# A spectral filter's 32-point transforms moved from TensorE to VectorE, inside an attention kernel

## The chip, the cores and the metric

One core of a Trainium2 chip. The metric is the device time of one execution in microseconds (us), the median of several runs. The engines run side by side and wait for one another by semaphores: TensorE (PE in the profile, its weight loads PEld), VectorE (DVE), ScalarE (ACT), GpSimd (POOL) and SyncE (SP), which here only issues DMAs.

## The reference

Two independent branches on 2048 x 448 inputs in float32, put side by side in the output: attention of 16 heads of 28 that share one key and one value head, and a filter in the frequency domain.

```python
def _A_ref(x, wq, wk, wv, wo):
    q = (x @ wq).reshape(B, S, H, Dh).transpose(0, 2, 1, 3)
    k = x @ wk
    v = x @ wv
    scores = jnp.einsum("bhqd,bkd->bhqk", q, k) * (Dh ** -0.5)
    p = _softmax(scores, axis=-1)
    o = jnp.einsum("bhqk,bkd->bhqd", p, v)
    return o.transpose(0, 2, 1, 3).reshape(B, S, H * Dh) @ wo

def _B_ref(x, w_r, w_i):
    X = jnp.fft.rfft2(x, axes=(-2, -1))
    X = X * (w_r + 1j * w_i)
    return jnp.fft.irfft2(X, (S, D), axes=(-2, -1))
```

The inputs A_wq and A_wk are drawn eight times as large as the other weights.

## The kernel before, in words

**Head.** TensorE projects x to queries, keys and values in four column chunks c of 512 queries, each in four groups g of four heads. Floats are split into a high and a low part and multiplied in two or three passes. Between the projections lie the first transforms of the filter (`fft1_fold`, `fft1_a`, `fft1_mm`, `fft1_out`), in eight portions q: the sequence of 2048 is cut into 64 x 32, and this step does the 448-point transform along the rows and the 64-point transform along the sequence. The result goes to the tile bs, and from there with two DMAs per q to the DRAM tensor t1. The keys are built in two halves (`keys(0)`, `keys(1)`), each moved into the tile ka by three DMAs. In the head only TensorE's order is written out; the order of the other engines and of SP's queue is made by the framework, by readiness and place in the program.

**Attention.** 16 groups (c, g), each of 16 steps (kc, 128 keys): 256 steps. A step is four score products into four PSUM banks (L696, out of a ring of six), four exponentials on ScalarE (L700) into tiles p, and four value products that run side by side in four column blocks of one bank, po (L678). TensorE does two steps of scores, then two steps of values. At the end of a group po is copied by VectorE (L686) and normalized in four parts (`norm`): the sum in every 29th row is spread over its 32 rows by a shuffle, inverted at full size and multiplied. `build_q` makes the next group's queries by three VectorE operations and nine DMAs. PSUM has eight banks: six for scores, one for fillers (aux), one for po.

**Fillers.** Between the scores of a pair of steps TensorE takes one unit of other work, by a table (`mid`, `at`): first the filter's 32-point transforms, forward (`fft2_a`) and back (`fft2_b`) as products with a 128 x 128 matrix in three split passes, the product with the filter on VectorE between them; from t1 and to t2, both in DRAM. Then the last transforms (`fft3_a`, `fft3_b`, from t2 to the output ob), and for each chunk c the output projection (`wo_unit`, L598) in 16 units. The last chunk's projection and the last group's normalization form the tail.

Of the kernel before, what the change touches and what calls it, by code (L numbers as in the profile page):

```python
# [1 line left out]

# [18 lines left out]
DH = D // H  # L21
DF = D // 2 + 1
NG = 4
# [5 lines left out]
BANKS = 6  # L29
O_BUFS = 1  # L30
X_BUFS = 1
P_BUFS = 8
LAG = 1
TAIL = 0
# [4 lines left out]
def kernel(ctx: ExitStack, tc: tile.TileContext, t: dict):  # L39
# [4 lines left out]
    dp = ctx.enter_context(tc.tile_pool(name="dp", bufs=1, space=DRAM))  # L44
    fp = ctx.enter_context(tc.tile_pool(name="fp", bufs=2))
    qp = ctx.enter_context(tc.tile_pool(name="qp", bufs=2))
# [11 lines left out]
    t1 = dp.tile([128, 32, DF], F32, name="t1")  # L58
    t2 = dp.tile([128, 32, DF], F32, name="t2")

# [6 lines left out]
    aux_pool = [None]  # L67

    def aux(name):
        return aux_pool[0].tile([128, 512], F32, name=name, tag="aux")  # L70

    def aux2(name):
        return aux_pool[0].tile([128, 2, DF], F32, name=name, tag="aux")

    fc, xb, ff = {}, {}, {}
    ps1 = [None]

    def fft1_consts():
        fc["cs1"] = fp.tile([128, 4, 113], F32, name="cs1", tag="cs", bufs=1)
        nc.sync.dma_start(fc["cs1"], t["cs1"])

    def fft1_load(q):
        if q > 7:
            return
        x = fp.tile([128, 4, 256], F32, name="xb", tag=("wr", "b2")[q % 2])
        nc.sync.dma_start(x, t["xb"][q])
        w = fp.tile([128, 4, 64], F32, name="fw", tag=("fi", "z0")[q % 2])  # L90
        nc.sync.dma_start(w, t["fw"][:, 4 * q:4 * q + 4])
        xb[q] = x, w

    def fft1_fold(q):
        x = xb[q][0][:113]
        f = ff[q] = fp.tile([113, 4, 4, 2, 32], F32, name="f", tag="wi")
# [12 lines left out]
    at1, stored = {}, []  # L109

    def fft1_a(q, ps=range(2)):
        f, cs1 = ff[q], fc["cs1"][:113]
        for p in ps:
            pa = ps1[0].tile([128, 2, DF], F32, name="pa", tag="p")
# [7 lines left out]
            a = at1[q, p] = fp.tile([128, 2, DF], F32, name="a", tag=("pwr", "pwi")[p])  # L122
            nc.scalar.activation(a, pa, AF.Copy)
# [4 lines left out]
    def fft1_mm(q):  # L128
        w = xb[q][1]
        pb = aux2("pbb"), ps_o.tile([128, 2, DF], F32, name="po")  # L130
# [8 lines left out]
    def fft1_out(q, pb, after=None):  # L139
        bs = fp.tile([128, 2, 2, DF], F32, name="bs", tag=("cst", "cst", "wr", "b2")[q // 2])  # L140
# [7 lines left out]
        for e in range(2):  # L148
            n0 = 16 * e + 2 * q
            stored.append(nc.sync.dma_start(t1.rearrange("(l s) n f -> s l n f", l=2)[:, :, n0:n0 + 2],  # L150
                                            bs[64 * e:64 * e + 64]))

    def fft2_consts():
        for n in ("g1", "g2"):
            g = fp.tile([128, 128], F32, name=n, tag="g", bufs=1)
            nc.gpsimd.dma_start(g, t[n])
            h = fc[n + "h"] = fp.tile([128, 128], F32R, name=n + "h", bufs=1)
            l = fc[n + "l"] = fp.tile([128, 128], F32R, name=n + "l", bufs=1)
            nc.gpsimd.tensor_copy(h, g)
            nc.gpsimd.tensor_tensor(l, g, h.bitcast(F32), op=ALU.subtract)  # L160

    qa = {}
# [10 lines left out]
    def build_q(c, g, first=False):  # L173
        cs = slice(c * CW, (c + 1) * CW)
        qt = qp.tile([128, CW], F32, name="qt", bufs=1)
        qh = qp.tile([128, CW], F32R, name="qh", bufs=1)
        ql = qp.tile([128, CW], F32R, name="ql", bufs=1)
# [3 lines left out]
        if (c, g) not in qa:  # L181
            qa[c, g] = qp.tile([128, 4, CW], F32R, name="qa")
        q = qa[c, g]
        if first:
            return q, qh, ql
        for i in range(4):
            for p, src in enumerate((qh, ql)):
                mv = nc.sync.dma_start(q[32 * p:32 * p + 32, i].bitcast(F32), src[32 * i:32 * i + 32].bitcast(F32))
                behind(mv, stored[-1])
# [3 lines left out]
    ps_x = ctx.enter_context(tc.tile_pool(name="ps_x", bufs=X_BUFS, space=PSUM))  # L193
    ps_o = ctx.enter_context(tc.tile_pool(name="ps_o", bufs=O_BUFS, space=PSUM))
    aux_pool[0] = ps_x


    with tc.tile_pool(name="w1", bufs=1) as w1, tc.tile_pool(name="p1", bufs=6, space=PSUM) as p1:
        ps1[0] = p1
# [30 lines left out]
        def shift(c0, c1):  # L230
            pb = p1.tile([128, NG, c1 - c0], F32, name="pb2", tag="p")
# [4 lines left out]
        with tc.tile_pool(name="x1", bufs=2) as x1:  # L236
# [6 lines left out]
            for n in WARM:  # L243
                nothing = p1.tile([128, 512], F32, name="nothing", tag="p")
# [54 lines left out]
            slots = (3, 5, 6, 8, 9, 10)  # L299
# [6 lines left out]
            def key_max():  # L306

                nc.vector.tensor_reduce(qm, qmx[:, 0:2], axis=AX.X, op=ALU.max)
                pb = p1.tile([128, 64], F32, name="pb", tag="p")
# [5 lines left out]
            pqs = [p1.tile([128, 512], F32, name="pq", tag="p") for _ in range(NG)]  # L315
# [16 lines left out]
            sgn = const("sgn", [128, 1], nc.sync)  # L332
# [7 lines left out]
            for c in range(1, NC):  # L340
                for g in range(NG):
                    pq = p1.tile([128, 512], F32, name="pq", tag="p")
# [22 lines left out]
                    if n in slots:  # L365
                        q = slots.index(n)
# [24 lines left out]
        pb3 = p1.tile([128, 64], F32, name="pb3", tag="p")  # L391
# [6 lines left out]
        pv = p1.tile([128, 16, 32], F32, name="pv", tag="p")  # L398
# [8 lines left out]
        with tc.If(rv > int(np.float32(BOUND).view(np.int32))), tc.tile_pool(name="g1", bufs=1) as g1:  # L407
# [9 lines left out]
            banks = [p1.tile([128, 512], F32, name="ps", tag="p") for _ in range(2)]  # L417
            with tc.For_i(0, 64, 1) as n:
# [3 lines left out]
                for i in range(4):  # L422
                    r = slice(32 * i, 32 * i + 32)
                    for h in range(4):
                        ps = banks[0]
                        mm(ps, qs[r], k4[r, h * 512:(h + 1) * 512], start=True, stop=True)
                        nc.vector.tensor_reduce(mx[:, i, h:h + 1], ps, axis=AX.X, op=ALU.max)
# [21 lines left out]
    ps_s = ctx.enter_context(tc.tile_pool(name="ps_s", bufs=1, space=PSUM))  # L449
    ring = [ps_s.tile([128, CW], F32, name=f"s{i}") for i in range(BANKS)]  # L450
# [3 lines left out]
    begun = []  # L454
    woh = ap.tile([128, NG, D], F32R, name="woh", bufs=1)
    wol = ap.tile([128, NG, D], F32R, name="wol", bufs=1)

    def wo_split(g):
        w = ap.tile([128, D], F32, name="wo", tag="ya")
        behind(nc.gpsimd.dma_start(w, t["wo"][:, g]), begun[-1])  # L460
# [4 lines left out]
    def mm3(out, w, h, l):  # L465
        mm(out, fc[w + "h"], h, start=True, stop=False)  # L466
        mm(out, fc[w + "l"], h, start=False, stop=False)  # L467
        mm(out, fc[w + "h"], l, start=False, stop=True)  # L468

    b2 = {}  # L470

    t1v = t1.rearrange("(l r h) n f -> r l n h f", r=2, l=2)

    def fft2_load(q):
        b = b2["b", q] = fp.tile([128, 4, DF], F32R, name="b2", tag="b2")
        for r in range(2):
            for l in range(2):
                p = (r * 2 + l) * 32
                ld = nc.sync.dma_start(b[p:p + 32].bitcast(F32), t1v[r, l][:, 4 * q:4 * q + 4])
                behind(ld, begun[-1])  # L480
        for n in ("wr", "wi"):
            b2[n, q] = fp.tile([128, 4, DF], F32, name=n)
            for r in range(2):
                ld = nc.gpsimd.dma_start(b2[n, q][64 * r:64 * r + 64], t[n][:, 4 * q:4 * q + 4])
                behind(ld, begun[-1])

    pr, cst = {}, {}

    def fft2_split(u):
        q, v = divmod(u, 2)  # L490
        b = b2["b", q][:, 2 * v:2 * v + 2]
        bh = b2["h", u] = fp.tile([128, 2, DF], F32R, name="bh", bufs=1)
        nc.vector.tensor_copy(bh, b.bitcast(F32))  # L493
        nc.vector.tensor_tensor(b, b.bitcast(F32), bh.bitcast(F32), op=ALU.subtract)

    def fft2_a(u):
        q, v = divmod(u, 2)
        s = slice(2 * v, 2 * v + 2)
        b, wr, wi = (b2[n, q][:, s] for n in ("b", "wr", "wi"))
        pu = aux2("pu")  # L500
        mm3(pu, "g1", b2["h", u], b)
        pf, p2 = fp.tile([128, 2, DF], F32, name="pwr"), fp.tile([128, 2, DF], F32, name="pwi")
        nc.vector.tensor_tensor(pf, pu, wr, op=ALU.mult)
        nc.vector.tensor_tensor(p2[0:64], pu[64:128], wi[64:128], op=ALU.mult)
        nc.vector.tensor_tensor(p2[64:128], pu[0:64], wi[0:64], op=ALU.mult)
        nc.vector.scalar_tensor_tensor(pf, p2, sgn, pf, op0=ALU.mult, op1=ALU.add)
        h = fp.tile([128, 2, DF], F32R, name="ph", bufs=1)
        nc.vector.tensor_copy(h, pf)
        p = fp.tile([128, 2, DF], F32R, name="pl", bufs=1)
        nc.vector.tensor_tensor(p, pf, h.bitcast(F32), op=ALU.subtract)  # L510
        pr[u] = h, p

    def fft2_b(u):
        v = u % 2
        pc = aux2("pc")
        mm3(pc, "g2", *pr.pop(u))
        if v == 0:
            cst[0] = fp.tile([128, 4, DF], F32, name="cst")
        nc.vector.tensor_copy(cst[0][:, 2 * v:2 * v + 2], pc)
        if v:  # L520
            nc.sync.dma_start(t2[:, 2 * u - 2:2 * u + 2], cst[0])


    def fft3_consts():
# [330 lines left out]
```

## Time and profile before

| what | value |
|---|---|
| median of three runs | 671.88 us (671.17 to 674.48) |
| span of the profiled execution | 669.5 us |
| TensorE busy | 660.4 us, 4480 products |
| ScalarE busy | 560.4 us |
| VectorE busy | 319.8 us |
| GpSimd busy | 63.4 us |
| DMA | 61.86 MB, 34250 packets |
| granted TensorE clock | 1.000 |

The span runs from the first to the last instruction of one profiled execution; the runs' times are taken without the profile and hold what lies around the span too. A line of a timeline has the start, the duration and the engine, then the program's line, the operation, the tiles (written <- read), the shape and the number of instructions that were merged, and in brackets the idle time before it with the one who ended it. SPq marks a DMA issue on SP's queue: the duration is that of the issue, not of the transfer. In the groups of lines the last columns are the busy time, the mean ns of one, and the idle time of the engine just before.

### The profile page before, as it was taken

What the parts mean: (1) busy time and instruction counts of PE and PEld (TensorE: products, weight loads), DVE (VectorE), ACT (ScalarE), POOL (GpSimd) and SP (SyncE); (2) the same over time, 40 slices, a digit from 0 to 9 for tenths busy, and PEclk for the clock granted to TensorE, in tenths of its full rate; (3) what the DMA queues carried; (4) which work ended last, traced back from release to release, by engine and by line L of the source; (5) the groups of instructions that cost most, each with busy time, mean ns of one, the idle gap of its engine ahead of it and who ended that gap; (6) DMA issues with size and microseconds to landing.
All of it is one profiled execution on the core that took longest, in us unless ns stands there. A gap on an engine that the chain in (4) does not pass through costs nothing.

```text
span 669.5 us, 11846 instructions
## 1 busy us (share of the span) xinstructions
PE 660.4 (99%) x4480; PEld 371.3 (55%) x4480; DVE 319.8 (48%) x771; ACT 560.4 (84%) x1117; POOL 63.4 (9%) x113
## 2 busy tenths in 40 slices
PE   8999899999999999999999999999999999999997
PEld 6877545555555555555555555555555555555555
DVE  5999537759995912045342502073514220071613
ACT  4554898988988988988898988899898998898882
POOL 3022202322110000000001100000100100000110
PEclk9999999999999999999999999999999999999999
DMA  8765755656452323030322222020423220120001
GB/s 261 257 170 169 208 147 140 146 149 163 136 139 83 79 83 78 15 77 15 83 80 60 74 70 54 22 70 15 121 56 89 77 69 23 46 60 1 28 29 56
DMA packets 34250, 61.86 MB, mean 92 GB/s; under 512 B 6529, under 2 KB 22802, under 8 KB 33228
## 3 DMA queue, kind: packets, MB, share of 16 engines
q1 hardware_dynamic: 30544, 49.18, 26.6%
q0 software_dynamic: 3072, 11.00, 6.4%
q8 instruction: 36, 0.59, 0.4%
q10 hardware_dynamic: 576, 0.92, 0.4%
q14 instruction: 22, 0.18, 0.1%
HBM read 29.35 MB, written 14.75 MB: 66 GB/s over the span
## 4 chain that ended last, share of the span: by engine, by line
PE 88%; DVE 1%; ACT 0%; ACTq 0%; issue 0%; DVEq 0%
PE s L696 39%; PE po L678 35%; PE pw L598 5%; PE py L560 2%; PE pz L546 2%; PE s L598 1%; PE pu L468 0%; PE pc L466 0%; PE pc L468 0%; PE pc L467 0%; PE pu L466 0%; PE pu L467 0%; ACT yb L603 0%; DVE bs L145 0%; DVE kl L222 0%; PE s L735 0%
## 5 line engine op out<-in xcount | busy, mean ns | idle before, releaser
L700 ACT ACTIVATE p<-s 128x512 f32<-128x512 f32 x1024 | 517.5, 629 | 62.8 <-PE s L696 62.5
L696 PE MATMUL s<-qa,ka 128*128 128x512 f32 x1024 | 297.6, 413 | 0.6 <-ACT vs L402 0.6
L696 PEld LDWEIGHTS s<-qa,ka 128*128 128x128 f32 x1024 | 179.4, 188 | 135.5 <-ACT p L700 107.6
L678 PE MATMUL po<-p,vs 128*32 128x512 f32 x2048 | 246.3, 599 | 2.0 <-DVE bs L145 2.0
L678 PEld LDWEIGHTS po<-p,vs 128*32 128x32 f32 x2048 | 53.6, 109 | 124.9 <-issue 117.2
L605 DVE COPY ya<-pw 128x448 f32<-128x448 f32 x12 | 7.5, 624 | 145.5 <-PE pw L598 128.0
L586 DVE RECIPROCAL r<-r 128x128 f32<-128x128 f32 x64 | 60.7, 949 | 1.2
L569 POOL TENSOR_TENSOR yo<-y 128x226 f32<-128x226 f32 x16 | 9.3, 582 | 432.4 <-issue 291.5
L566 DVE TENSOR_TENSOR y<-py,m 128x226 f32<-128x226 f32 x16 | 6.3, 394 | 62.2 <-ACT m L564 62.2
L549 DVE COPY z<-pz 113x512 f32<-113x512 f32 (+1 forms) x16 | 11.1, 691 | 48.5 <-PE pz L546 48.4
L291 PE MATMUL pq<-xh,wqh 128*128 128x512 f32 x64 | 26.0, 406 | 1.1 <-ACT wqh L273 1.1
L291 PE MATMUL pq<-xh,wql 128*128 128x512 f32 x64 | 25.2, 394 | 0.3 <-DVE wql L274 0.2
L295 ACT ACTIVATE qraw<-pq 128x512 f32<-128x512 f32 x16 | 9.2, 600 | 18.4 <-PE pq L291 18.4
L493 DVE CAST bh<-b 128x450 fp32r<-128x450 f32 x16 | 6.4, 397 | 36.7 <-PE pu L467 22.2
L686 DVE COPY osb<-po 128x512 f32<-128x512 f32 x15 | 10.3, 689 | 21.4 <-PE po L678 21.4
L585 DVE STREAM_SHUFFLE r<-osb 128x128 f32<-128x128 f32 x64 | 19.0, 297 | 0.1
L587 DVE TENSOR_TENSOR osb<-osb,r 128x128 f32<-128x128 f32 x64 | 18.4, 287 | 1.2
L291 PE MATMUL pq<-xl,wqh 128*128 128x512 f32 x48 | 18.8, 392 | 0.0
L598 PE MATMUL pw<-woh,ol 128*128 128x448 f32 x51 | 18.7, 368 | 0.0
L598 PE MATMUL pw<-wol,oh 128*128 128x448 f32 x51 | 18.6, 364 | 0.0
L598 PE MATMUL pw<-woh,oh 128*128 128x448 f32 x51 | 18.4, 362 | 0.0
L560 PEld LDWEIGHTS py<-cs,z 113*128 113x128 f32 (+1 forms) x128 | 17.4, 191 | 1.7
(124 smaller groups left out, 555.4 us busy)
## 6 DMA issues: line engine op xcount, KB each, us to landing
qa<-qa SPq DMA_DIRECT2D x15, 512.0 KB, 4.3
raw<-xa SPq DMA_DIRECT2D x16, 256.0 KB, 5.4
xb<-xb SPq DMA_DIRECT2D x8, 512.0 KB, 3.7
qa<-qh SPq DMA_DIRECT2D x60, 64.0 KB, 2.1
qa<-ql SPq DMA_DIRECT2D x60, 64.0 KB, 2.0
ob<-yo SPq DMA_DIRECT2D x16, 226.0 KB, 2.0
t<-bs SPq DMA_DIRECT2D x16, 225.0 KB, 3.5
wr<-wr POOLq DMA_DIRECT2D x16, 225.0 KB, 5.1
```

The source lines that it names most:

```text
L291: mm(pq, w[:, j, gs], x[:, j], start=(j == 0 and n == 0), stop=(j == 3 and n == 1))
L546: mm(pz[:w, j], c2["c", q][:, j, o0:o0 + w], c2["F", q][:, j], start=True, stop=True)
L549: nc.vector.tensor_copy(z[:w], pz[:w].rearrange("p j (r n) -> p r j n", r=2))
L560: mm(py[:, k], z[:w, r, js], cs3[:w, k], start=True, stop=True)
L585: nc.vector.stream_shuffle(r, o, [DH] * 32)
L586: nc.vector.reciprocal(r, r)
L587: nc.vector.tensor_tensor(o, o, r, op=ALU.mult)
L598: mm(p, x[c][:, g, s], w[:, g], start=(g == 0 and n == 0), stop=(g == NG - 1 and n == 2))
L678: mm(po[c, g][32 * i:32 * i + 32], vs[:, kc], ps[i // 2][:, i % 2], start=(kc == 0), stop=(kc == 15))
L686: nc.vector.tensor_copy(o, po[c, g])
L696: last = mm(ring[b + j], ka[:, kc * 128:(kc + 1) * 128], qa[c, g][:, 2 * u + j], start=True, stop=True)
L700: nc.scalar.activation(p[:, j], ring[b + j], AF.Exp, scale=SCALE)
```

## The change

- **The 32-point transforms.** `fft1_out` writes into a tile X in SBUF (128 x 32 points x 2 x 113) in place of t1, by sixteen DMAs per q. VectorE does the forward transform on X in place, as five levels of butterflies (`plain`, `quarter`, `turn_by` and `update`), the product with the filter, and five levels back. A rotation by a quarter turn leaves real and imaginary rows exchanged (`turned`). `store` writes each q of the last level to t2 by eight or sixteen DMAs. The products `fft2_a`, `fft2_b` and their splits go.
- **The normalization.** The 512 x 4 sums of a group are written to DRAM, read back spread over 128 partitions, inverted in one operation of 128 x 16, written back, and read as a broadcast by four DMAs (`group_out`, `group_sums`, `group_norm`).
- **The order.** All eight banks are allocated once: seven for scores and fillers, taken by the time they come free, bank 7 for the values. TensorE, VectorE, ScalarE and SP are issued in an order from a model of time in the program (`clk`, `free`, `after`, `vector`). Values come in turns of two steps, or of three where fillers are waiting. VectorE's butterflies are background work that the model takes up whenever no due event is left. `partial` puts the last chunk's products of three groups ahead of the last values where the model sees TensorE waiting.
- **Beside it.** The tiles p become 20 single ones; the first transforms get tiles of their own; bs shares two buffers with the filter's loads; the copies m and the last sums yo move from ScalarE and GpSimd to VectorE.

The core of the diff:

```diff
 def fft1_out(q, pb, after=None):
-        bs = fp.tile([128, 2, 2, DF], F32, name="bs", tag=("cst", "cst", "wr", "b2")[q // 2])
+        bs = fp.tile([128, 2, 2, DF], F32, name="bs")
...
-        for e in range(2):
-            n0 = 16 * e + 2 * q
-            stored.append(nc.sync.dma_start(t1.rearrange("(l s) n f -> s l n f", l=2)[:, :, n0:n0 + 2],
-                                            bs[64 * e:64 * e + 64]))
+            for e in range(2):
+                n = 16 * e + 2 * q
+                for r in range(2):
+                    for u, w in ((0, 113), (1, 112)):
+                        k = 64 * u + 32 * h
+                        nc.sync.dma_start(X[k:k + 32, n:n + 2, r, :w],
+                                          bs[64 * e + 32 * r:64 * e + 32 * r + 32, h, :, 113 * u:113 * u + w])
...
+    clk = {"pe": 0.0, "dve": 4.0, "act": 0.0, "mode": "s", "new": False}
+    def vector(until):
+        while clk["dve"] < until:
+            if events and events[0][0] <= clk["dve"]:
+                _, _, dur, f, a = heapq.heappop(events)
+                clk["dve"] += dur
+                f(*a)
+            elif background:
+                dur, f = background.popleft()
+                clk["dve"] += dur
+                f()
+            else:
+                clk["dve"] = min(until, events[0][0]) if events else until
+    def wide(n):
+        return 0.12 + 0.00108 * n
...
+    def plain(a, b, n):
+        def first():
+            TT(flat(a), flat(a), flat(b), op=ALU.add)
+        def second():
+            STT(flat(b), flat(b), -2.0, flat(a), op0=ALU.mult, op1=ALU.add)
+        for f in first, second:
+            background.append((wide(226 * n), f))
...
+    def forward():
+        m, lv = 16, 0
+        while m:
+            for j in range(16 // m):
+                a = 2 * m * j
+                w = np.exp(-1j * np.pi * _rev(j, lv) * m / 16)
+                for sa, sb, n in cut(a, a + m, m):
+                    if j == 0:
+                        plain(sa, sb, n)
+                    elif j == 1:
+                        quarter(sa, sb, n, -1)
+                    else:
+                        k = big(w)
+                        turn_by(sb, w, k, 0, n, True)
+                        update(sa, sb, 0, n, float(k))
+            m, lv = m // 2, lv + 1
...
+    def store(q):
+        d = [turned[q + 8 * j] for j in range(4)]
+        runs = [(0, 4, 1)] if len(set(d)) == 1 else [(0, 3, 1), (3, 4, 1)] if q == 0 else [(0, 4, 2), (1, 4, 2)]
+        for j0, j1, st in runs:
+            s = slice(q + 8 * j0, q + 8 * (j1 - 1) + 1, 8 * st)
+            for r in range(2):
+                for l in range(2):
+                    for u, w in ((0, 113), (1, 112)):
+                        p = 64 * u + 32 * l
+                        nc.sync.dma_start(t2w[r, l][:, 4 * q + j0:4 * q + j1:st, 113 * u:113 * u + w],
+                                          X[p:p + 32, s, r ^ d[j0], :w])
+        if q == 7:
+            for k in range(2):
+                after(clk["dve"], 0.0, fft3_load, k)
...
+    def fft3_load(q):
+        nc.sync.dma_start(c2t[q % 2], t2[:, 4 * q:4 * q + 4])
+        nc.gpsimd.dma_start(fit[q % 2], t["fi"][:, 4 * q:4 * q + 4])
+        after(clk["dve"] + 5.0, 0.0, work["z"].extend, [z_unit(q, 0), z_unit(q, 1)])
...
+    def group_out(c, g):
+        o = osb[c, g] = qraw[:, g, c * CW:c * CW + CW]
+        V.tensor_copy(o, bank[7])
+        taken_out[0] += 1
...
+        nc.sync.dma_start(sd, o[DH::32])
+        nc.sync.dma_start(rs, sd.rearrange("i (a b) -> (i a) b", b=16))
+        after(clk["dve"] + 5.5, 0.3, group_sums, c, g, rs, rd)
...
+    def values(o, n):
+        while taken_out[0] < o // 16:
+            vector(clk["dve"] + 0.5)
+        switch("v")
+        for st in range(o, o + n):
+            c, g, kc = steps[st]
+            for i in range(4):
+                mm(bank[7][32 * i:32 * i + 32], vs[:, kc], pt.pop(4 * st + i), start=(kc == 0), stop=(kc == 15))
+            clk["pe"] = max(clk["pe"], end[4 * st + 3]) + 0.86
+            if kc == 15 and st < 255:
+                after(clk["pe"] + 0.4, 0.72, group_out, c, g)
...
+    background.append((0.0, lambda: [filter_load(k) for k in range(2)]))
+    forward()
+    for k in range(8):
+        filters(k)
+    inverse()
```

More of the change, by code (lines that the diff above doesn't have):

```diff
@@ L487 @@
[L487 to L511, printed above, removed]
@@ new lines, in partial, with size @@
+    def partial():
+        k, g = parts.popleft()
+        if g == 0:
+            b = min(range(7), key=free.__getitem__)
+            clk["pe"] = max(clk["pe"], free[b])
+            free[b] = inf
+            tail[k] = bank[b][:, :D]
+        switch("s")
+        wo_mm(tail[k], NC - 1, k, (g,))
+        spent(0.605)
+    def size():
+        left = 16 - done_steps % 16
+        rich = sum(map(len, work["w"])) * 0.6 + len(work["z"]) * 0.88 > 1.0
+        return left if left < 4 else 2 if left == 4 or not rich else 3
```

675 lines of the change are left out of this document (407 added, 268 removed).

## The prediction

> **What bounds the kernel now.** I read the page first: busy shares, then the chain that ended last, then the costliest group.
>
> ```profile
> span 669.5 us, 11846 instructions
> PE 660.4 (99%) x4480; PEld 371.3 (55%) x4480; DVE 319.8 (48%) x771; ACT 560.4 (84%) x1117; POOL 63.4 (9%) x113
> PE 88%; DVE 1%; ACT 0%; ACTq 0%; issue 0%; DVEq 0%
> L700 ACT ACTIVATE p<-s 128x512 f32<-128x512 f32 x1024 | 517.5, 629 | 62.8 <-PE s L696 62.5
> ```
>
> TensorE holds 88% of the chain, and ScalarE's only idle time in the exponentials (62.5 us) is waiting for scores. A busy TensorE alone proves little, so I went to its timeline for the price of one pair of steps, first without and then with a filler (a piece of the filter or of the output projection put between the scores).
>
> ```profile
> 72.11 1.17 PE L696 MATMUL s<-qa,ka 128*128 128x512 f32 x4 [0.57 <-ACT vs L402]
> ...
> 77.36 1.07 PE L678 MATMUL po<-p,vs 128*32 128x512 f32 x8 [2.03 <-DVE bs L145]
> ...
> 86.22 2.18 PE L696 MATMUL s<-qa,ka 128*128 128x512 f32 x8
> ...
> 94.14 1.20 PE L696 MATMUL s<-qa,ka 128*128 128x512 f32 x4
> 95.18 0.36 PE L466 MATMUL pu<-bh,g1h 128*128 128x450 f32 x1
> ...
> 96.81 1.92 PE L678 MATMUL po<-p,vs 128*32 128x512 f32 x16
> 98.67 1.20 PE L696 MATMUL s<-qa,ka 128*128 128x512 f32 x4
> ...
> 302.47 1.20 PE L696 MATMUL s<-qa,ka 128*128 128x512 f32 x4
> ...
> 307.00 1.20 PE L696 MATMUL s<-qa,ka 128*128 128x512 f32 x4
> ...
> 644.41 1.20 PE L696 MATMUL s<-qa,ka 128*128 128x512 f32 x4
> ...
> 649.22 2.18 PE L696 MATMUL s<-qa,ka 128*128 128x512 f32 x8
> ...
> 651.33 3.64 PE L678 MATMUL po<-p,vs 128*32 128x512 f32 x32
> 78.89 19.81 ACT L700 ACTIVATE p<-s 128x512 f32<-128x512 f32 x40 [2.16 <-PE s L696]
> ```
>
> From 86.22 to 94.14 lie two pairs without a filler: 3.96 us each. With a unit of the 32-point transforms a pair takes 98.67 - 94.14 = 4.53, with a unit of the projection (302.47 to 307.00) 4.53, with a unit of the last transforms (644.41 to 649.22) 4.81. So 128 pairs cost 128 x 3.96 = 506.9, the 32 + 48 units 80 x 0.57 = 45.6, the 32 last ones 32 x 0.85 = 27.2: 579.7, against 582.9 from the first score (72.1) to the end of the last values (651.33 + 3.64). The stage is a sum of TensorE's work. ScalarE's floor is near: 40 exponentials take 19.81, so (19.81 - 0.63) / 39 = 0.49 each and 3.93 per pair.
>
> **What the change takes off TensorE.** The 32 units of the 32-point transforms go: 32 x 0.57 = 18.2. Turns of three steps, where fillers are plentiful, leave out two of eight switches between scores and values in a group of 16 steps; 16 passes of values without a switch take 3.64 - 1.92 = 1.72, and 1.86 lie between 96.81 and 98.67, so a switch costs 0.14 on the values' side. With as much on the scores' side and at most 12 such groups that is 24 x 0.28 = 6.7 at most, none at least; I take 5, near the upper end, because both sides change. At the tail:
>
> ```profile
> 654.97 5.67 PE s L598 x27
> 660.64 1.82 PE pw L598 x9
> ...
> 662.00 0.29 DVE L587 TENSOR_TENSOR osb<-osb,r 128x128 f32<-128x128 f32 x1
> 664.56 0.92 PE L735 MATMUL pw<-w,osb 128*128 128x448 f32 x2
> 665.75 0.54 ACT L603 ACTIVATE yb<-pw 128x448 f32<-128x448 f32 x1 [0.45 <-PE pw L735]
> ```
>
> The 36 partial products (7.5 us) move ahead, into waits of TensorE for the last exponentials. But VectorE's normalization ends at 662.29 either way, and one product and its copy follow it (about 0.9 + 0.3 before the copy begins, at 663.5 where it is 665.75): 2.3 is gained, not 7.5. Without any new wait: 669.5 - 18.2 - 5 - 2.3 = 644.0 of span. The median of the runs, 671.9, is 2.4 above this execution's span; I add that 2.4 at the end and count it as lying around the span.
>
> **What it adds to SyncE's queue.** This part decides. The first transform's results went to DRAM in two DMAs for each of eight q; now they go into the tile X in sixteen (e, h, r and the two halves), 32 partitions each, SBUF to SBUF, 128 in all, all on SP. What SP needs for one is seen where several stand in a row:
>
> ```profile
> 215.89 0.59 SPq L188 DMA_DIRECT2D qa<-qh  x1
> 216.52 0.59 SPq L188 DMA_DIRECT2D qa<-ql  x1
> 217.16 0.59 SPq L188 DMA_DIRECT2D qa<-qh  x1
> ...
> 115.60 0.34 SPq L521 DMA_DIRECT2D t<-cst  x1
> 86.44 1.84 SPq L479 DMA_DIRECT2D b<-t  x4
> 43.18 1.38 SPq L150 DMA_DIRECT2D t<-bs  x2
> ...
> 51.03 1.43 SPq L224 DMA_DIRECT2D ka<-ka  x1
> 52.98 1.17 SPq L224 DMA_DIRECT2D ka<-kl  x2
> ...
> 57.72 4.52 SPq L215 DMA_DIRECT2D kf<-qraw  x7
> ...
> 75.01 0.68 SPq L224 DMA_DIRECT2D ka<-ka  x1
> qa<-ql SPq DMA_DIRECT2D x60, 64.0 KB, 2.0
> c<-t SPq DMA_DIRECT2D x32, 112.5 KB, 3.1
> 112.79 0.68 DVE L686 COPY osb<-po 128x512 f32<-128x512 f32 x1
> ```
>
> The moves qa<-qh are the nearest in form (SBUF to SBUF, 32 partitions): one every 0.63. The bounds: 0.46 (b<-t from DRAM, 32 partitions) and 0.69 (t<-bs); the whole-tile store t<-cst shows 0.34, but with 128 partitions and one run each. X's runs are 452 bytes, which moves little data, so I price the issue, not the bytes. 128 x 0.63 = 80.6 us of SP. It starts at 43.2, where the stores start now (the fw load ahead of them waits for the second transform either way). In between lie the two xb and two fw loads (2.0, at 0.5 each, between 0.34 and 0.69), the moves of both halves of the keys (3.1 as from 51.03 to 54.15, and 2.0 when nothing is waited for between the three) and the seven kf fetches (4.5): 11.6. The last X move is issued at 43.2 + 80.6 + 11.6 = 135.4 and lands by 137.4 (2.0 for a move).
>
> What is queued behind: the second half of the keys (75.0 now) stands behind seven of the eight q, 112 moves, and would leave at about 125, while step 8 wants it at about 90. ScalarE stands behind them too: bs has two buffers, so the copy of q waits for the moves of q - 2, and in its order follow the queries' parts. VectorE's level 0 needs q = 6 and 7 for its last quarter, its order is written out, and so everything after that quarter waits.
>
> Where this reaches TensorE: bank 7 must be copied out before the next group's values. The planner sets that copy on VectorE after about 27 us of butterflies by its own prices (0.12 + 0.00108 n): 8.8 of level 0, of which three quarters may run earlier, and 18 of the next levels. So 20 us of VectorE stand between X and the first copy-out: 137.4 + 20 = 157.4. The copy now starts at 112.79; without the four fillers before it (4 x 0.57 = 2.3) and the 2.0 that the first values wait at 77.36 it would be at 108.5. The shift is 48.9, and it stays: VectorE always has background work in the plan, so it is not made up. The late keys (125 + 2 + eight steps, 143) lie inside it. With 0.46 the shift is 27, with 0.69 it is 57.
>
> **VectorE's own work.** The code gives 274 operations on 109,384 elements for all butterflies and the product with the filter, 151 us at the planner's prices.
>
> ```profile
> 41.84 0.68 DVE L103 TENSOR_TENSOR xb<-f 113x512 f32<-113x512 f32 x1
> 42.55 0.42 DVE L104 TENSOR_TENSOR f<-xb 113x256 f32<-113x256 f32 x1
> 42.90 0.42 DVE L105 TENSOR_TENSOR f<-xb 113x256 f32<-113x256 f32 x1
> L506 DVE SCALAR_TENSOR_TENSOR pwr<-pwi,sgn,pwr 128x450 f32<-128x450 f32 x16 | 11.5, 718 | 0.0
> L586 DVE RECIPROCAL r<-r 128x128 f32<-128x128 f32 x64 | 60.7, 949 | 1.2
> ```
>
> An operation that the next one needs takes 0.71 at 512 elements (41.84 to 42.55; the planner has 0.67), one that it doesn't need 0.35 at 256 (planner 0.40). So the prices hold within a few per cent; the 200 operations with a scalar may cost up to 0.1 more (0.72 at 450), 0 to 13 us in all with the independent ones set against them. I take 0. In exchange 60 of the reciprocals go (57 us). Moving m and yo from ACT and POOL to VectorE adds under 20 us late, where it has room.
>
> **The stores before the last transforms.** 80 DMAs (eight or sixteen per q, by which rows are turned) leave within about 20 us of VectorE. At 0.46 SP needs 37 and ends 17 behind; the store's landing (2 to 3) and the load's 3.1 add about 6. The planner books 5.5 for it, and then a turn's end and six scores come first, about 10 in all; TensorE's order is fixed, so it waits 13. At 0.34 (27 of issue, 7 behind) it waits 3 or less. I take 6 of 0 to 13, because the planner may also find projection units to put first.
>
> The sum: 644.0 + 48.9 + 6 = 698.9, and 2.4 around it: **701 us**.
>
> The Trainium skill (DMA: Bandwidth & Descriptors, Issuing engines are not separate DMA queues) says that the sequencer's time to initiate a DMA is usually small relative to the DMA itself. By that rule the 128 moves would be hidden and the time would be that of the first rival below. This trace speaks against it for small moves: 0.59 of issue beside 2.0 to landing.
>
> **Rivals.**
> 1. *The issue of X's moves is cheap* (faster). At 0.34 plus 0.04 between two, as the whole-tile store shows, X is there at 43.2 + 48.6 + 11.6 + 2.0 = 105.4, the shift is 17 and the time 663; if it is hidden wholly, 646. It turns from faster to slower where one move takes SP about 0.45. For it: SP's queue idles much of the head now. Against it: no SBUF to SBUF move of this trace takes under 0.50. Chance 0.27.
> 2. *In between*: a move at about 0.46 and no wait for the stores gives 644.0 + 27 + 2.4 = 673, no change. Chance 0.06.
> 3. *VectorE becomes the bound by its rate*, X being in time: the scalar operations at 0.1 more put the copy-outs 13 late, 644.0 + 13 + 2.4 = 659. VectorE's order holds no gap in the first 180 us for it. I count it inside rival 1's chance; on top of the forecast it gives 714.
> 4. *ScalarE becomes the bound*: 128 x 3.93 = 503 stays under TensorE's 560 in the stage, so only the stretch without fillers is level. It changes nothing.
>
> **How the numbers follow.** The forecast's case, SP as the bound, has 0.67: the price of a move is seen 120 times, and what waits for it follows from written-out orders. Its own range is 679 (0.46 a move, 6 for the stores) to 719 (0.69 a move and 13 for the stores give 716, and a few more for VectorE's scalar operations). The whole range must reach down to rival 1, of whose cases only the wholly hidden one is left out: 648 to 719. Half a per cent, 3.4 us, is about what a measurement of this kernel can tell from no change. Slower 0.67, same 0.06, faster 0.27.
>
> **What would show it.** In the profile after: SP's rows X<-bs, near 0.6 each and back to back from about 43 to 135; ka<-kl near 125 in place of 76; TensorE idle after the eighth step with a DMA of ka as releaser, and again at the first values of the second group with VectorE as releaser; VectorE's first rows on X waiting for X<-bs. Then pairs near 3.96 while the butterflies run, with no pu or pc. The prediction is wrong if X<-bs takes under 0.45 each, or if X lands before 100: then the end is below 665.

## The result, and the profile after

| | before | after |
|---|---|---|
| median of the runs | 671.52 us (4 runs, 670.27 to 674.48) | 747.63 us (4 runs, 746.69 to 751.87) |
| span of the profiled execution | 669.5 us | 744.9 us |

The change makes the kernel slower: ratio 1.1147 (95% interval 1.1107 to 1.1188). The forecast was slower, at 701 us; the measured time is 46.6 above it and above the range's end of 719.

The page of the kernel after, its busy shares, its granted clock in 40 slices and its chain:

```profile
span 744.9 us, 11810 instructions
PE 666.8 (90%) x4384; PEld 372.7 (50%) x4384; DVE 328.7 (44%) x649; ACT 550.7 (74%) x1101; POOL 30.3 (4%) x52
...
PE   8987657949898979987299999999999999999997
...
PEclk9996656978999989999699999999999999999999
...
PE 62%; DVE 13%; SPq 12%; DMA 9%; issue 3%; ACT 1%; ACTq 0%; DVEq 0%; POOLq 0%
```

TensorE had 88% of the chain before. Now VectorE and SP's queue (SPq) have 13% and 12% of it. TensorE idles 78.1 us (744.9 - 666.8), 73.5 of them in the first 20 slices. Its granted clock is down in many of these slices, too: in the view by windows it is 0.86 over the first half of the span and 1.00 over the second. SP's queue in the head, from the timeline:

```profile
42.12 11.61 SPq L154 DMA_DIRECT2D X<-bs  x16
...
54.93 10.24 SPq L154 DMA_DIRECT2D X<-bs  x16
...
68.99 10.30 SPq L154 DMA_DIRECT2D X<-bs  x16
79.34 4.41 SPq L205 DMA_DIRECT2D kf<-qraw  x7
83.85 44.33 SPq L154 DMA_DIRECT2D X<-bs  x64
128.28 0.56 SPq L214 DMA_DIRECT2D ka<-ka  x1
128.94 1.17 SPq L214 DMA_DIRECT2D ka<-kl  x2
130.20 10.39 SPq L154 DMA_DIRECT2D X<-bs  x16
```

The 128 moves take 86.9 us of issue, 0.68 each, from 42.1 to 140.6; between them SP issues other DMAs and hardly idles. VectorE, from its timeline:

```profile
142.08 1.10 DVE L498 TENSOR_TENSOR X<-X 128x904 f32<-128x904 f32 x1 [15.34 <-DMA X<-bs]
143.21 1.99 DVE L501 SCALAR_TENSOR_TENSOR X<-X 128x904 f32<-128x904 f32 x1
145.13 1.09 DVE L498 TENSOR_TENSOR X<-X 128x904 f32<-128x904 f32 x1
146.25 1.10 DVE L501 SCALAR_TENSOR_TENSOR X<-X 128x904 f32<-128x904 f32 x1
...
166.40 0.68 DVE L744 COPY qraw<-b 128x512 f32<-128x512 f32 x1
```

It waits for X until 142.08, 1.5 us after the last move is issued, and reaches the first copy-out (L744) at 166.40, where the prediction had 157.4. What TensorE waited for, the view of waits (total, times, longest):

```profile
PE b L136 <- ACT bs L144: 16.8, 4, 5.8
PE b L868 <- DVE qraw L744: 15.3, 4, 5.5
PE b L700 <- DMA X<-fi: 14.6, 1, 14.6
PE b L847 <- DVE ya L786: 7.5, 3, 3.8
PE b L847 <- DMA qa<-qa: 6.2, 1, 6.2
PE b L868 <- DVE bs L146: 5.6, 1, 5.6
PE b L136 <- DVE bs L146: 5.2, 1, 5.2
```

The rows on bs (27.6 together) belong to the head and the first group: bs has two buffers, and they come free only when SP has issued their moves and these have landed. In x_none below, which leaves the moves out, these rows are gone. The row on X<-fi and the rows on ya belong to the stretch from 321 to 390 us.

Against the prediction's no-wait sum of 644.0 the span has 100.9 too much: 57.9 until the first copy-out (166.4 where it would be 108.5; foreseen 48.9), and 43.0 later, of which 6 was foreseen. The experiments had to say what the 43 are, and whether the butterflies as such cost anything.

### The profile page after: what moved, and what is told of

Its sections match the earlier page's. It is cut to its first block, busy times and chain, and to the rows that moved or that the text cites. A ratio compares the mean times of both kernels' runs of the same rounds, so it can differ in the third digit from the quotient of the medians.

```text
span 744.9 us, 11810 instructions
## 1 busy us (share of the span) xinstructions
PE 666.8 (90%) x4384; PEld 372.7 (50%) x4384; DVE 328.7 (44%) x649; ACT 550.7 (74%) x1101; POOL 30.3 (4%) x52
## 4 chain that ended last, share of the span: by engine, by line
PE 62%; DVE 13%; SPq 12%; DMA 9%; issue 3%; ACT 1%; ACTq 0%; DVEq 0%; POOLq 0%
PE b L847 24%; PE b L868 22%; SPq L154 7%; PE b L281 5%; PE b L778 4%; SPq L660 2%; PE b L700 2%; DMA sd<-qraw 2%; PE b L719 2%; SPq L184 2%; DVE X L501 2%; DMA X<-bs 1%; PE b L121 1%; DVE X L549 1%; DMA qa<-ql 1%
## 5 line engine op out<-in xcount | busy, mean ns | idle before, releaser
L849 ACT ACTIVATE p<-b 128x512 f32<-128x512 f32 x1024 | 509.0, 643 | 120.8 <-PE b L847 120.8
L847 PE MATMUL b<-qa,ka 128*128 128x512 f32 x1024 | 293.6, 420 | 14.5 <-DVE ya L786 7.5
L868 PE MATMUL b<-p,vs 128*32 128x512 f32 x2048 | 251.2, 616 | 20.9 <-DVE qraw L744 15.3
L847 PEld LDWEIGHTS b<-qa,ka 128*128 128x128 f32 x1024 | 187.6, 194 | 146.8 <-issue 63.3
L868 PEld LDWEIGHTS b<-p,vs 128*32 128x32 f32 x2048 | 56.4, 111 | 151.5 <-issue 126.8
L744 DVE COPY qraw<-b 128x512 f32<-128x512 f32 x15 | 10.3, 689 | 117.1 <-PE b L868 117.1
L754 DVE RECIPROCAL rs<-rs 128x16 f32<-128x16 f32 x15 | 3.8, 253 | 65.6 <-DMA rs<-sd 65.6
L700 PE MATMUL b<-X 128*112 128x128 f32 (+1 forms) x128 | 17.5, 282 | 14.6 <-DMA X<-fi 14.6
L281 PE MATMUL b<-xh,wqh 128*128 128x512 f32 x64 | 27.3, 427 | 0.8 <-ACT wqh L263 0.8
L281 PE MATMUL b<-xh,wql 128*128 128x512 f32 x64 | 26.6, 415 | 0.1
L766 DVE TENSOR_TENSOR qraw<-qraw,R 128x512 f32<-128x512 f32 x15 | 10.3, 689 | 30.9 <-DMA R<-rd 30.4
L778 PE MATMUL b<-woh,oh 128*128 128x448 f32 x60 | 22.5, 375 | 0.0
L552 DVE SCALAR_TENSOR_TENSOR X<-w,X 128x452 f32<-128x452 f32 (+2 forms) x37 | 21.9, 592 | 1.2
L549 DVE SCALAR_TENSOR_TENSOR X<-w,X 128x452 f32<-128x452 f32 (+2 forms) x37 | 21.9, 592 | 1.2
L778 PE MATMUL b<-wol,oh 128*128 128x448 f32 x60 | 22.1, 369 | 0.0
```

The costliest lines, as they stand in the source:

```text
L281: mm(pq, w[:, j, gs], x[:, j], start=(j == 0 and n == 0), stop=(j == 3 and n == 1))
L549: STT(flat(b), tw[0][:, o:o + n], -k, flat(a), op0=ALU.mult, op1=ALU.add)
L552: STT(flat(a), tw[0][:, o:o + n], k, flat(a), op0=ALU.mult, op1=ALU.add)
L700: mm(pz[:w, j], c2t[q % 2][:, j, o0:o0 + w], fit[q % 2][:, j], start=True, stop=True)
L778: mm(p, x[c][:, g, s], w[:, g], start=(g == 0 and n == 0), stop=(g == NG - 1 and n == 2))
L847: mm(bank[b], ka[:, kc * 128:(kc + 1) * 128], qa[c, g][:, h], start=True, stop=True)
```

## Experiments

Two theories were open from the start. **S**: SP's issue of small moves sets the time; what is queued behind them comes late. **D**: the order that the program's model of time wrote out takes DMA round trips as shorter than they are, so that VectorE stands at an operation whose data is still under way. The main rivals: VectorE is too slow for the butterflies, or the small packets load the DMA engines. Where no range is given below, the kernel ran once; gains over the change are differences of spans.

**x_none**: X is zeroed, and its 128 moves are left out.

```diff
-    nc.gpsimd.memset(X[64:128, :, :, 112], 0.0)
+    nc.gpsimd.memset(X, 0.0)
...
-                        nc.sync.dma_start(X[k:k + 32, n:n + 2, r, :w], ...)
+                pass
```

> The 128 moves into X are left out (X is set to zero once, so the filter's branch computes on zeros); all else is as in the changed kernel. Theory S (SyncE needs 0.64 us to issue each move, and the head, the second half of the keys and the first butterflies wait behind that queue): the first copy-out of bank 7 comes near 109 us in place of 167, and the span falls by about 58, to 687; the waits after the second group (about 40 us in all) stay. Theory V (the butterflies on VectorE are too slow for the plan): the span stays within 10 us of 745, because every butterfly is still there. Theory B (the 8192 runs of 452 bytes are slow on the DMA engines, not on SyncE): as S here; the next two runs tell it from S.

Measured: 694.57 us, span 692.8, first copy-out at 110.5. The moves cost 52 us of the span (58 expected), all of it before the first copy-out, which comes 56 earlier. Theory V is out: it foresaw at most 10, as every butterfly is still there. The time is still 23 above before: X is not all of it.

**x_pool**: half of the moves issued by GpSimd; bytes and packets stay.

```diff
-                        nc.sync.dma_start(X[k:k + 32, n:n + 2, r, :w],
+                        (nc.gpsimd if h else nc.sync).dma_start(X[k:k + 32, n:n + 2, r, :w],
```

> Half of the moves into X (h = 1, 64 of 128) are issued by GpSimd, the other half by SyncE; the same runs of bytes go over the same engines. S: SyncE saves 64 x 0.64 = 41 us of issue; X is complete at about 105 in place of 142, the first copy-out near 130 in place of 167, the span near 708. B: the same packets take the same time, the span stays within 10 of 745. V: the same, within 10 of 745.

Measured: 713.89 us, span 712.1, first copy-out at 131.7. The same transfers, issued from two queues, bring the first copy-out 35 us earlier: the issue set the time, not the packets. The change's own trace agrees, since X is there 1.5 us after the last of its moves is issued.

**x_dram**: X by way of a DRAM tensor, 16 stores and 32 loads, 24 of these on GpSimd.

```diff
+            nc.sync.dma_start(t1.rearrange("(l s) n f -> s l n f", l=2)[:, :, n0:n0 + 2], bs[64 * e:64 * e + 64])
+        if q % 4 == 3:
...
+                            (nc.sync if q == 7 and e == 0 else nc.gpsimd).dma_start(
+                                X[k:k + 32, n:n + 8, r, :w],
+                                t1[64 * l + 32 * r:64 * l + 32 * r + 32, n:n + 8, 113 * u:113 * u + w])
```

> The first transform's results go through DRAM: two stores per q on SyncE as in the kernel before, and 32 loads into X (24 of them on GpSimd's queue), again in 8192 runs of 452 bytes. SyncE issues 24 DMAs in place of 128. S: SyncE saves about 65 us; X is complete at 85 to 95, the first copy-out comes at 112 to 120, and the span is 692 to 702. B: more bytes move than before and as many short runs, so the span stays above 735. V: within 10 of 745.

Measured: 709.81 us (709.43 to 710.46), ratio 1.0568 (1.0542 to 1.0594), span 708.0, first copy-out at 126.6. That is 36.9 less than the change, but less of a gain than expected: VectorE's order still holds butterflies ahead of the first copy-out for which X is not there. It waits 3.1 us and then 10.3 us at them, until 98.6 (the trace names qa<-qh, a move on the same queue, for the second wait, but the operation reads X alone). The last load of X is issued by 90.2. From 88 to 103 us the 16 DMA engines are full in the view by windows (share 0.99 and more, where the change has 0.13 to 0.23), so this way the transfers probably hold X back, not only the issue; that was not tested.

**x_hold**: as x_dram, and the model places no butterfly before 27 us of its clock.

```diff
-            elif background:
+            elif background and clk["dve"] >= 27.0:
```

> As x_dram (X filled by way of DRAM, in 16 stores and 32 loads), and besides the planner places no butterfly before 27 us of its own clock, so that VectorE does not stand in its order at a butterfly whose rows of X have not come. In x_dram the first copy-out came at 126.6 us, with VectorE waiting 3.1 us for X and 10.3 us for a projection load in the order. Theory: first copy-out at 109 to 112 us, span about 691 to 695. Rival: butterflies held back crowd later groups; the first copy-out is earlier but the later groups grow by as much, and the span stays near 708.

Measured: 689.11 us (688.67 to 691.75), ratio 1.0260 (1.0238 to 1.0282), span 690.0, first copy-out at 116.2. As expected but for the copy-out, which came 4 to 7 later: TensorE itself waits 4.1 us for a move of the queries shortly before it. VectorE still waits 9.2 us for X.

**sums_late**: the change, with the two round trips of the sums booked at 9.5 us in the model, not 5.5.

```diff
-        after(clk["dve"] + 5.5, 0.3, group_sums, c, g, rs, rd)
+        after(clk["dve"] + 9.5, 0.3, group_sums, c, g, rs, rd)
...
-        after(clk["dve"] + 5.5, 1.8, group_norm, c, g, R)
+        after(clk["dve"] + 9.5, 1.8, group_norm, c, g, R)
```

> Only the planner's delays change: 9.5 in place of 5.5 us for each of the two DMA round trips of a group's sums, so that VectorE's written-out order has more butterflies ahead of the inversion and of the product. Theory D (VectorE stands idle 5.4 to 7.5 us per group at the inversion because its order books 5.5 us for two DMAs that take about 11, and this lag reaches TensorE at the group's end): groups 1 to 3 shrink from 36 us to 32 or 33, and the span falls by 8 to 12. Rival R (VectorE's rate alone sets these groups): the waits at the inversion vanish from VectorE's rows, but the groups stay at 35 to 36 and the span within 3 us.

Measured: 733.31 us (730.72 to 733.56), ratio 1.0918 (1.0891 to 1.0944), span 728.9: 16 less, where 8 to 12 were expected. The next four groups take 32.3, 31.3, 33.0 and 32.9 us, where the change has 36.1, 35.8, 37.1 and 35.3. The timelines of VectorE and SP in the change show why the trip is long:

```profile
202.49 0.68 DVE L744 COPY qraw<-b 128x512 f32<-128x512 f32 x1
...
208.44 0.40 DVE L552 SCALAR_TENSOR_TENSOR X<-w,X 128x226 f32<-128x226 f32 x1
214.25 0.25 DVE L754 RECIPROCAL rs<-rs 128x16 f32<-128x16 f32 x1 [5.42 <-DMA rs<-sd]
```

```profile
201.92 0.56 SPq L184 DMA_DIRECT2D qa<-qh  x1
...
206.34 0.59 SPq L184 DMA_DIRECT2D qa<-ql  x1
208.41 0.50 SPq L185 DMA_DIRECT2D qa<-qa  x1
208.96 0.54 SPq L749 DMA_DIRECT2D sd<-qraw  x1
212.66 0.34 SPq L750 DMA_DIRECT2D rs<-sd  x1
214.53 0.34 SPq L755 DMA_DIRECT2D rd<-rs  x1
```

The sums are copied out by 203.17, but their store stands on SP behind the next group's queries and leaves at 208.96. From there to the reciprocal 5.3 us pass, about the 5.5 that the model booked. The 5.8 before it, SP's queue, are not in the model, and VectorE's wait is of their size, 5.42. It is so in the first five groups of the change: the store leaves 5.8 to 7.5 us after the copy, and VectorE waits 5.4 to 7.5 at the reciprocal. So here D is S again: for a free queue the booking would have been about right.

**recip_back**: the change, its reciprocals put back on VectorE.

```diff
-        nc.sync.dma_start(sd, o[DH::32])
-        nc.sync.dma_start(rs, sd.rearrange("i (a b) -> (i a) b", b=16))
-        after(clk["dve"] + 5.5, 0.3, group_sums, c, g, rs, rd)
+        for k in range(4):
+            after(clk["dve"], 1.25, group_recip, c, g, k, R)
+        after(clk["dve"], 1.8, group_norm, c, g, R)
...
+    def group_recip(c, g, k, R):
+        s = slice(128 * k, 128 * k + 128)
+        V.stream_shuffle(R[:, s], osb[c, g][:, s], [DH] * 32)
+        V.reciprocal(R[:, s], R[:, s])
```

> The change with only its reciprocals put back on VectorE (four shuffles and reciprocals of 128x128 per group, 5.0 us) and no round trip of the sums; X moves and stores as in the change. If the waits for rs and R, and not VectorE's own operations, lengthened groups 1 to 4: these take 31 to 33 us instead of 36 as in sums_late, span about 729 (725 to 733). Rival: VectorE's 5 us more per group fill the room, groups stay at 36, span 740 to 748.

Measured: 723.86 us (723.44 to 724.98), ratio 1.0781 (1.0755 to 1.0807), span 721.7: 23.2 less than the change, more than sums_late gave, and a little better than expected. The next four groups take 32.4, 31.4, 31.1 and 33.8 us. The seven DMAs per group leave SP's queue with the round trips, so the 23.2 hold what stood behind them, too. The stretch from 167.1 to 311.4 us in the view by windows (length, then busy time and instructions of each engine, PEclk, DMA share, GB/s), first of the change, then of recip_back:

```profile
167.10:311.40 144.30, 134.53 (x776) 62.97 (x777) 116.77 (x225) 125.12 (x255) 3.25 (x6) 0.94 0.23 57
```

```profile
167.10:311.40 144.30, 144.03 (x867) 70.75 (x868) 134.17 (x265) 135.85 (x277) 3.24 (x6) 0.98 0.24 60
```

VectorE does 17.4 us more in the same time, and TensorE gets 9.5 us more busy and 91 more products through. It was VectorE's waits that slowed these groups, not its work.

**z_late**: the units of the first two loads of the last transform (z) given 30 us in the model, not 5.

```diff
-        after(clk["dve"] + 5.0, 0.0, work["z"].extend, [z_unit(q, 0), z_unit(q, 1)])
+        after(clk["dve"] + (30.0 if q < 2 else 5.0), 0.0, work["z"].extend, [z_unit(q, 0), z_unit(q, 1)])
```

> The planner gives the first two inverse units (z) as available 30 us after their loads are queued instead of 5. Theory S/D, that orders by hand are laid for shorter DMA round trips than they take: TensorE's wait of 14.6 us for X<-fi at 370 us goes, and the span falls from 744.9 to about 730. Rival: the data of those stores is late for all that follows, the wait only moves to a later z unit or to the copy-out, and the span stays within 4 us of 744.9.

Measured: 747.84 us, span 746.1. The rival was right: the wait for X<-fi is gone, and 13.3 us of wait for ya stand at 384 us in its place. SP in the change, and under it VectorE and SP in z_late, show what both have in common:

```profile
337.24 23.27 SPq L660 DMA_DIRECT2D t<-X  x48
360.61 0.38 SPq L788 DMA_DIRECT2D oa<-ya  x1
361.03 3.87 SPq L660 DMA_DIRECT2D t<-X  x8
364.94 2.07 SPq L690 DMA_DIRECT2D X<-t  x2
```

```profile
356.60 0.69 DVE L744 COPY qraw<-b 128x512 f32<-128x512 f32 x1 [8.37 <-PE b L868]
383.35 0.25 DVE L754 RECIPROCAL rs<-rs 128x16 f32<-128x16 f32 x1 [26.06 <-DMA rs<-sd]
383.52 0.56 DVE L786 COPY ya<-b 128x448 f32<-128x448 f32 x1
```

```profile
377.98 0.54 SPq L749 DMA_DIRECT2D sd<-qraw  x1
```

Behind 48 stores in a row stands the load of the z unit (X<-t); the unit's other load, X<-fi, is GpSimd's and waits for the same stores. The sums stand behind them too. In z_late they are copied out by 357.29, but their store leaves SP only at 377.98, and VectorE stands at the reciprocal for 26.06 us. The copy to ya, which frees a bank of TensorE, comes right behind in VectorE's order. In the change it is the same on a smaller scale: no copy to ya waits for a DMA of its own there, they come behind waits for rs (5.71) and R (6.82 and 5.12).

**st_pool**: half of these stores issued by GpSimd.

```diff
-                        nc.sync.dma_start(t2w[r, l][:, 4 * q + j0:4 * q + j1:st, 113 * u:113 * u + w],
+                        (nc.gpsimd if l else nc.sync).dma_start(t2w[r, l][:, 4 * q + j0:4 * q + j1:st, 113 * u:113 * u + w],
```

> Half of the 128 stores of the products (t<-X) go to GpSimd's queue, nothing else is changed. If SyncE's issue of them (48 moves in 23.3 us) sets the phase: SyncE's block ends some 18 us earlier, TensorE's wait for X<-fi (14.6 us) falls to about 3, those for ya (3.3 and 3.8 us) go, and the span falls by 15 to 20 us, to 725 to 730. Rival: ya waits for VectorE's own order and the landing of a load bounds X<-fi; then at most 5 us are gained.

Measured: 738.08 us, span 736.3: 8.6 less, half of what was expected and more than the rival's 5. (There are 80 of these stores, not 128; 40 went to GpSimd.) The wait for X<-fi falls from 14.6 to 5.7; of the waits for ya 4.8 and 1.2 remain.

**cures_nox**: sums_late, st_pool and 12 us for the first z units together; X as in the change.

```diff
-        after(clk["dve"] + 5.0, 0.0, work["z"].extend, [z_unit(q, 0), z_unit(q, 1)])
+        after(clk["dve"] + (12.0 if q < 2 else 5.0), 0.0, work["z"].extend, [z_unit(q, 0), z_unit(q, 1)])
```

The lines of sums_late and st_pool are the same as above.

> All cures but the one for X: the change with its 128 moves of X on SyncE, sums booked at 9.5 us, half of the product stores on GpSimd, z units given 12 us. If the three shares add up: first copy-out at about 167 us as in the change, groups 1 to 4 at 31 to 33 us, span 744.9 less 16 (sums) less 9 to 20 (stores and z), 709 to 720, some 55 to 60 over all_fixed. Rival: the late first group has pushed work together that the cures cannot spread; then over 725.

Measured: 712.63 us, span 710.9, first copy-out at 166.4, the next four groups 32.5, 31.3, 33.1 and 33.1. Sums, stores and z together give 34.0 of the 43.0 beyond the first group. That is 9 more than 16.0 and 8.6: both lots of DMAs stand in the same queue, so one cure can help the other, and the z units' later booking is in it too; that was not separated.

**all_fixed**: cures_nox and x_hold together, with no line that these two don't have:

```diff
-                        nc.sync.dma_start(X[k:k + 32, n:n + 2, r, :w], ...)
+            for e in range(2):
+                nc.sync.dma_start(t1..., bs[64 * e:64 * e + 64])
...
-            elif background:
+            elif background and clk["dve"] >= 27.0:
...
-        after(clk["dve"] + 5.5, 0.3, group_sums, c, g, rs, rd)
+        after(clk["dve"] + 9.5, 0.3, group_sums, c, g, rs, rd)
...
```

> All cures together: X by way of DRAM, butterflies held until 27 us, sums' round trips booked at 9.5 us, half of the product stores on GpSimd, z units given 12 us. If the excess over the no-wait sum of 644.0 is made of the X moves (58 us in the first group), of the sums' waits (15) and of the store phase (26), the span is 645 to 665 and the kernel is faster than the one before (671.7). Rival: the butterflies themselves cost VectorE more than the units cost TensorE, and the span stays over 672 with the waits gone.

Measured: 654.97 us (650.67 to 658.25), ratio 0.9739 (0.9684 to 0.9795): faster than before, and as expected. Span 655.1; X's share, against cures_nox, is 55.8.

**norm_dve**: as all_fixed, with the reciprocals on VectorE as in recip_back:

```diff
-        after(clk["dve"] + 9.5, 0.3, group_sums, c, g, rs, rd)
+        for k in range(4):
+            after(clk["dve"], 1.25, group_recip, c, g, k, R)
...
```

> As all_fixed, but the reciprocals are made on VectorE as in the kernel before (shuffle of 128x128 at 0.30 us and reciprocal at 0.95, four of each per group: 5.0 us), in place of the sums' round trips through DRAM. If the DMA form is what lets VectorE carry the butterflies: VectorE, busy 116 of 129 us in groups 1 to 4 of all_fixed, gets some 20 us more there, these groups grow from 31 to 33 us to about 36, and the span is 10 to 20 us longer than all_fixed's 655, at 665 to 675. Rival: VectorE makes up for it in the later groups, where it is busy about a quarter of the time; then within 4 us of 655.

Measured: 650.39 us (647.51 to 652.54), ratio 0.9678 (0.9642 to 0.9714). I had expected 10 to 20 us more than all_fixed; its median is 4.6 below, with intervals that overlap. It is not slower, and beats both kernels. Its page:

```profile
span 648.7 us, 11774 instructions
PE 640.0 (99%) x4384; PEld 358.5 (55%) x4384; DVE 396.6 (61%) x814; ACT 548.8 (85%) x1101; POOL 67.4 (10%) x116
...
PE 83%; DMA 4%; SPq 1%; ACT 0%; issue 0%; DVE 0%; ACTq 0%
```

TensorE's longest waits in it, and the view by windows over groups with butterflies:

```profile
PE b L848 <- DMA qa<-qa: 1.6, 1, 1.6
PE b L137 <- ACT bs L145: 1.1, 1, 1.1
```

```profile
113.60:242.50 128.90, 128.90 (x788) 62.65 (x787) 120.20 (x239) 127.16 (x260) 3.90 (x7) 1.00 0.21 54
```

VectorE is busy 120.2 of 128.9 us there and TensorE never idles. Butterflies and reciprocals both fit, so the way of the sums through DRAM has nothing to pay for.

**tuned**: all_fixed with 20 us for every z unit.

```diff
-        after(clk["dve"] + (12.0 if q < 2 else 5.0), 0.0, work["z"].extend, [z_unit(q, 0), z_unit(q, 1)])
+        after(clk["dve"] + 20.0, 0.0, work["z"].extend, [z_unit(q, 0), z_unit(q, 1)])
```

> As all_fixed, with all z units given 20 us after their loads are queued instead of 12 and 5. all_fixed has one wait left of over 3 us after the first group, 5.46 us at 317.7 for a z unit's X. Expected: it goes, span 648 to 655. Rival: the z units bunch at a later place and the wait appears there for ya, span 655 to 662.

Measured: 653.61 us (648.32 to 656.84), ratio 0.9704 (0.9660 to 0.9747), span 655.1. The wait of 5.46 at 317.7 is gone and the span is the same; the first copy-out, which this edit does not touch, came at 117.0 where all_fixed has 112.9. These runs cannot tell the two apart.

## Why the prediction was wrong

The direction and its main term came true: the change is slower, and the largest part is the first copy-out, held up by SP's issue of X's moves: 57.9 late where 48.9 was foreseen. What failed is the rest: 43.0 after the first copy-out, where the sum has 6. The step behind more than half of it is the 0 for the sums' round trips.

- **The no-wait sum, 644.0.** As a whole it is borne out: norm_dve, with X and the stores cured, the sums made on VectorE and no wait of TensorE over 1.7 us, has a span of 648.7. Its three parts were not tested one by one. Between two waits the pairs of the change take 3.91 (173.34 to 177.25), about as foreseen (3.96).
- **SP's price of a move: right, a little low.** 0.68 measured, 0.63 taken; the last is issued at 140.6, not 135.4, and X is there at 142.1, not 137.4. The second half of the keys leaves at 128.3 (foreseen about 125), but the wait for it is hidden: TensorE was late by then through bs, which the prediction named for ScalarE and did not price for TensorE.
- **From X to the first copy-out: 20 taken, 24.3 measured.** 3.3 of the difference are five operations between 143 and 153 us that took longer than their like (1.99 beside 1.10 in the rows above). Why is not settled. With the 4.7 of X this makes the shift 57.9 in place of 48.9. x_none (110.5, where the no-wait sum has 108.5) and x_pool show that nearly all of the shift is SP's issue.
- **VectorE's own work: the step that failed.** The prices held (1.10 at 904 elements is the planner's 1.10). What I left out is the round trip that the change adds to each group's sums. I counted the 57 us of reciprocals as a gain and put no price on the DMAs that take their place, nor on their place in SP's queue behind the queries. VectorE waits 65.6 us for rs and 30.4 for R in the whole run, the later part of it with time to spare. The term is 16.0 by sums_late and 23.2 by recip_back, where 0 stood.
- **The stores before the last transforms: 6 taken, of 0 to 13.** 39.3 us of issue for 80 stores were foreseen well (37). But I followed only the load of z behind them. The sums' DMAs stand there too, and by VectorE's order a wait for them delays the copy to ya, which holds a bank. In recip_back, which has no such DMAs, TensorE's waits for ya are gone, while the 14.6 for X<-fi stay. With the sums' later booking in place the stores and z still give 18.0 (cures_nox against sums_late).
- **A term that was missing: TensorE's clock.** The 4384 products of the change are busy 666.8 us, those of norm_dve 640.0. So of the 96.2 us between these spans 69.4 are TensorE standing still and 26.8 are as many products taking longer, at a mean granted clock of 0.931 against 0.991.

The sizes that were left out all have one sign, so the range, built on terms of 6 and 0 beside the main one, ended too low. Of the rivals, the first (663 or less with X in time) did not come true either: without any move of X, x_none still takes 694.57.

The Trainium skill's rule (DMA: Bandwidth & Descriptors, Issuing engines are not separate DMA queues), by which the sequencer's time is usually small relative to the DMA itself, does not hold for these moves: x_pool, which changes nothing but the issuing engine of half the moves, takes the kernel from 747.63 to 713.89 us.

## What to carry to other kernels

Price each small DMA as work of the queue that issues it, and walk down that queue: whatever stands behind it, for whatever other purpose, is late by the sum. A hand-made order has to book a DMA's round trip from the moment when its queue gets to it, not from the moment when the data is ready. An operation that is slow but local (here 5 us of reciprocals per group on an engine with room) can beat a cheap one with two round trips.

## What the runs showed of the hardware

A wait of TensorE costs more than its length. Two group starts of the change, from the timeline:

```profile
167.14 3.64 PE L868 MATMUL b<-p,vs 128*32 128x512 f32 x16 [5.54 <-DVE qraw L744]
170.71 2.71 PE L847 MATMUL b<-qa,ka 128*128 128x512 f32 x8
173.34 1.92 PE L868 MATMUL b<-p,vs 128*32 128x512 f32 x16
175.20 2.12 PE L847 MATMUL b<-qa,ka 128*128 128x512 f32 x8
177.25 1.92 PE L868 MATMUL b<-p,vs 128*32 128x512 f32 x16
...
239.01 2.46 PE L868 MATMUL b<-p,vs 128*32 128x512 f32 x16 [2.99 <-DVE qraw L744]
241.41 3.15 PE L847 MATMUL b<-qa,ka 128*128 128x512 f32 x8
```

After 5.54 us of wait 16 products take 3.64 where 1.92 is usual, and the next eight 2.71 where it is 2.12: 2.3 us on top of the wait. After 2.99 it is 1.6. The granted clock in the view by windows goes with it: 0.50 from 166.5 to 171.0, 0.83 to 174.0, 1.00 to 180.0; and 0.82 from 238.0 to 241.5, 0.69 to 245.0, 1.00 to 250.0. Shorter waits were enough, too: after 2.46 us at 203.23 the next 16 products take 3.34 (clock 0.57 from 203.2 to 206.6), and in tuned, after 1.88 us at 214.62, they take 3.24 (0.57 from 214.6 to 217.9). After 1.23 us at 209.96 in all_fixed they take the usual 1.92. Over the change's groups from 167.1 to 311.4 us the clock is 0.94, over norm_dve's from 113.6 to 242.5 it is 1.00.

The Trainium skill (TensorE: Matmul & The Clock Gate, Part 1: The HAM clock gate) says that the clock halves after an idle window of about 3.4 us, doubles again after about as much work, and that the ramp, which it describes for a kernel's start, costs under 1% of a typical span. The halving and the return agree with these rows; the length of the wait does not, as 1.88 us were enough. Where the waits come again and again, as here, the price is larger: 26.8 of 744.9 us are 3.6%.
